# AV on the diagonal as two matmuls of half the queries, and router data laid out by expert, then tile

## The chip, the cores and the metric

The kernel runs on one core of a Trainium2 chip. The metric is the time of one execution on the device, in microseconds. Each core has a matrix engine (TensorE, PE in the profile, its weight loads PEld), a vector engine (VectorE, DVE), an engine for functions of one operand (ScalarE, ACT), GpSimd (POOL), which here issues most of the DMAs, and SyncE (SP), which issues the rest.

## The reference, cut to what matters

```python
# attention: batch 8, heads 8, seq 576, head_dim 64
block = 64
scores = scale * np.matmul(q, k.transpose(0, 1, 3, 2))
mask = pos[:, None] // block >= pos[None, :] // block     # causal by blocks of 64
scores = np.where(mask, scores, -1e9)
attn = softmax(scores);  x = attn @ v                      # -> 4608 tokens of 512
# mixture of 8 experts, two for each token
noisy_logits = x @ w_gate + np.log1p(np.exp(x @ w_noise)) * noise
top2 = np.argpartition(-noisy_logits, 2, axis=1)[:, :2]
out[t] = sum over its two experts e of  weight * (relu(x[t] @ w1[e]) @ w2[e])
```

Within a block of 64 queries everything is seen up to the block's own 64 keys. So in a diagonal square of 128 keys by 128 queries one quarter is masked: the later 64 keys against the earlier 64 queries.

## The kernel before, in words

The work has two stages. In the first, the attention of all heads and the routing are done; in the second, sixteen blocks of an expert's tokens run through the two layers.

**Attention.** The batches are taken in four groups `g` of two batches each; a batch is one half of the 128 partitions while scores are made (`hf`). A group has two sets `st` of four heads (`SET`). A set has thirteen score units (`score_unit`): a unit makes scores on TensorE (L299) in one of two PSUM buffers (`sc`) and turns them into exp values on ScalarE (L302), which go to the tile `esc`; the thirteenth makes the last 64 keys (L310, L313, `esc4`). Scores lie with the keys on the partitions and the queries along the row, so that `esc` is used as it is as the stationary operand of the AV matmul. For key tile `jt` of 128 keys, the columns from `EO[jt]` on hold the queries from that tile's first on. The first 128 of them are the diagonal square. Its masked quarter is partitions 64 to 127 by the first 64 columns, and `score_unit` clears it with four memsets on VectorE at the end of a set (L316).

**AV.** `av_tile` computes one tile of 128 queries for four heads, in one of two PSUM buffers (`av`): tile `idx` below 8 is batch `hf` and query tile `ib`, and sums `ib + 1` matmuls of 128 keys by 128 queries (L341), the last of them the diagonal one; the moving operand is the values with a column of ones (65 columns), so that the sum of the exps comes out as well. Tile 8 holds the last 64 queries of both batches, in halves of 64 columns (L352). VectorE then takes the reciprocal (L356) and multiplies (L357) into `xr`.

**Routing.** `x_transpose` turns `xr` (L373) and copies it (L374); `router` is a generator of sixteen steps: the logits (L388), exp, copy and log on ScalarE (L392 to L394), then a row of small VectorE operations that find each token's two experts (`oh`, L404 and L411), their mask `m` (L414), which of the two comes first (`ms`, L427 and L428), and by prefix sums a slot. Some of the small tiles are laid out with the nine token tiles outside and the eight experts inside (`p t e`), others, such as `oh_all` and `ms`, the other way (`p e t`), so some operations write or read with a step. `scatter` sends the rows to their slots in DRAM by indirect DMAs from GpSimd (L495).

**Order.** The order of the instructions on each engine is written out by hand (`tc.manual_schedule`). A loop over slots runs one score unit each (26 slots a group) and then what `at(slot, ...)` has put there. AV tiles of the first set of a group stand in slots 15 to 23 of that group, those of the second set in slots 0 to 8 of the next one (for the last group, in five slots close together after the end of the scores). Loads of q, k and v come from GpSimd's queue, in the same order.

**Experts.** `layer1` (L570, evicted at L573) and `layer2` (L582, L587, L592) run back to back over `SEQ`, with gathers (L610) and the output's scatter (L594) from GpSimd.

Of the kernel before, what the change touches and what calls it, by code (L numbers as in the profile page):

```python
# [8 lines left out]
F32 = mybir.dt.float32  # L9
BF16 = mybir.dt.bfloat16  # L10
I32 = mybir.dt.int32
AF = mybir.ActivationFunctionType
ALU = mybir.AluOpType
AX = mybir.AxisListType
# [5 lines left out]
def kernel(  # L20
# [12 lines left out]
    nc = tc.nc  # L33
# [3 lines left out]
    E = moe_w_gate.shape[1]  # L37
    F = moe_w1.shape[2]
    assert Dm == H * D and N == B * S
    P = 128  # L40
    DB = Dm // P
    FB = F // P
    NG = B // 2
    TG = 9
    NT = NG * TG
# [15 lines left out]
    EO = (0, 576, 1024, 1344)  # L61
# [29 lines left out]
    keep = ctx.enter_context(tc.tile_pool(name="keep", bufs=1))  # L91
# [10 lines left out]
    rt = low.enter_context(tc.tile_pool(name="rt", bufs=1))  # L102
# [26 lines left out]
    rowid_i = consts.tile([P, E, CT], I32)  # L129
    rowid = consts.tile([P, E, CT], F32)  # L130

    nz_all = keep.tile([P, NT, E], F32)
    xa = xa_pool.tile([P, DB, CAP], BF16)
    nzw = [xa.rearrange("p a b -> p (a b)")[0:B * TG, 1024 * i:1024 * (i + 1)].bitcast(F32) for i in range(2)]
    slots = keep.tile([P, NT, 2], I32)
# [149 lines left out]
    def score_unit(g, u):  # L285
        st, w = divmod(u, UN)
        if w == 0:
            escs[(g, st)] = (esc_pool.tile([P, SET, 2, ESC], BF16, tag="esc", name="esc"),
                             esc_pool.tile([P, SET, 64], BF16, tag="esc4", name="esc4"))
        esc, esc4 = escs[(g, st)]  # L290
        sc = sc_ps.tile([P, 2, 512], F32, tag="sc")
        if w < UN - 1:
            hh, piece = divmod(w, 3)
            h = st * SET + hh
            for jt, a, z, off in PIECES[piece]:
                for hf in range(2):
                    c0 = col0(hf, h)
                    sl = slice(64 * hf, 64 * hf + 64)
                    nc.tensor.matmul(out=sc[:, hf, off:off + z - a],  # L299
                                     lhsT=kT[sl, c0 + jt * P:c0 + jt * P + P],  # L300
                                     rhs=qT[sl, c0 + a:c0 + z], start=True, stop=True)
            ins = nc.scalar.activation(out=esc[:, hh, :, piece * 512:(piece + 1) * 512], in_=sc,  # L302
                                       func=AF.Exp, scale=scale)
        else:
            for hh in range(SET):
                h = st * SET + hh
                for hf in range(2):
                    c0 = col0(hf, h)
                    sl = slice(64 * hf, 64 * hf + 64)
                    nc.tensor.matmul(out=sc[sl, 0, hh * 64:(hh + 1) * 64],  # L310
                                     lhsT=kT[sl, c0 + 512:c0 + 576],
                                     rhs=qT[sl, c0 + 512:c0 + 576], start=True, stop=True)
            ins = nc.scalar.activation(out=esc4.rearrange("p a b -> p (a b)"), in_=sc[:, 0, 0:SET * 64],  # L313
                                       func=AF.Exp, scale=scale)
            for jt in range(4):
                nc.vector.memset(esc[64:128, :, :, EO[jt]:EO[jt] + 64], 0.0)  # L316
        anchors[g * UG + u] = ins.ins.name
        pace.append(ins.ins.name)

# [4 lines left out]
    def av_tile(g, st, idx, part=None):  # L324
        esc, esc4 = escs[(g, st)]
        vb = vt[g % 2]
        if g not in xrs:
            xrs[g] = xr_pool.tile([P, TG, DR], BF16, tag="xr", name="xr")
            nc.gpsimd.memset(xrs[g][:, :, Dm + 2 * NREC:DR], 0.0)
            nc.gpsimd.tensor_copy(xrs[g][:, :, Dm + 4:Dm + 6].bitcast(I32)[:, :, 0], tokm[:, g, :])  # L330
        xr = xrs[g]
        if part != 1:
            avs_open[idx] = av_ps.tile([P, SET, D + 1], F32, tag="av", name="av")
        av = avs_open[idx]
        for hh in (range(SET) if part is None else range(2 * part, 2 * part + 2)):
            h = st * SET + hh
            if idx < 8:
                hf, ib = divmod(idx, 4)
                for jt in range(ib + 1):
                    c = EO[jt] + (ib - jt) * P  # L340
                    nc.tensor.matmul(out=av[:, hh, :], lhsT=esc[:, hh, hf, c:c + P],  # L341
                                     rhs=vb[:, 4 * hf + jt, h, :], start=(jt == 0), stop=(jt == ib))
            else:
                for jt in range(5):
                    for hf in range(2):
                        sl = slice(64 * hf, 64 * hf + 64)
                        if jt < 4:
                            c = EO[jt] + (4 - jt) * P
                            lhsT, rhs = esc[:, hh, hf, c:c + 64], vb[:, 4 * hf + jt, h, :]
                        else:  # L350
                            lhsT, rhs = esc4[sl, hh, :], vb[sl, 8, h, :]
                        nc.tensor.matmul(out=av[sl, hh, :], lhsT=lhsT, rhs=rhs,  # L352
                                         start=(jt == 0), stop=(jt == 4))
        if part != 0:
            rden = small.tile([P, SET, 1], F32, tag="rden")
            nc.vector.reciprocal(rden, av[:, :, D:D + 1])  # L356
            ins = nc.vector.tensor_tensor(  # L357
                out=xr[:, idx, st * SET * D:(st + 1) * SET * D].rearrange("p (h d) -> p h d", h=SET),
                in0=av[:, :, 0:D], in1=rden.to_broadcast([P, SET, D]), op=ALU.mult)
            if g == NG - 1 and st == 1:  # L360
                pace.append(ins.ins.name)
# [19 lines left out]
    def router(g):  # L381
        half, t0 = g // 2, g * TG
        lg = av_ps.tile([P, TG, 2 * E], F32, tag="av")
        for idx in range(TG):
            if idx in (3, 6):
                yield
            for db in range(DB):
                nc.tensor.matmul(out=lg[:, idx, :], lhsT=xts[g][:, idx, db, :], rhs=wgn[:, db, :],  # L388
                                 start=(db == 0), stop=(db == DB - 1))
        sp = rt.tile([P, TG, E], F32, tag="sp")  # L390
        lgs = rt.tile([P, TG, E], F32, tag="lgs")
        nc.scalar.activation(out=sp, in_=lg[:, :, E:2 * E], func=AF.Exp)  # L392
        nc.scalar.activation(out=lgs, in_=lg[:, :, 0:E], func=AF.Copy)
        nc.scalar.activation(out=sp, in_=sp, func=AF.Ln, bias=1.0)  # L394
        yield
        noisy = rt.tile([P, TG, E], F32, tag="noisy")
        nc.vector.tensor_mul(noisy, sp, nz_all[:, t0:t0 + TG, :])
        nc.vector.tensor_add(noisy, noisy, lgs)
        yield
        mx = rt.tile([P, 2, TG, 1], F32, tag="mx")  # L400
        nc.vector.reduce_max(mx[:, 0, :, 0], noisy, axis=AX.X)
        oh = oh_all[:, g]
        ohv = [oh[:, i].rearrange("p e t -> p t e") for i in range(2)]
        nc.vector.tensor_tensor(out=ohv[0], in0=noisy, in1=mx[:, 0].to_broadcast([P, TG, E]),  # L404
                                op=ALU.is_equal)
        yield
        nc.vector.scalar_tensor_tensor(out=noisy, in0=ohv[0], scalar=-1.0e30, in1=noisy,
                                       op0=ALU.mult, op1=ALU.add)
        nc.vector.reduce_max(mx[:, 1, :, 0], noisy, axis=AX.X)
        yield  # L410
        nc.vector.tensor_tensor(out=ohv[1], in0=noisy, in1=mx[:, 1].to_broadcast([P, TG, E]),  # L411
                                op=ALU.is_equal)
        m = rt.tile([P, TG, E], BF16, tag="m")
        nc.vector.tensor_add(m.rearrange("p t e -> p e t"), oh[:, 0], oh[:, 1])  # L414

        w2 = rt.tile([P, TG], F32, tag="w2")
        nc.vector.tensor_sub(w2, mx[:, 0, :, 0], mx[:, 1, :, 0])
        yield

        c2 = rt.tile([P, TG, E], F32, tag="lgs")  # L420
# [2 lines left out]
                                     data1=m.rearrange("p t e -> p (t e)"), initial=0.0,  # L423
                                     op0=ALU.mult, op1=ALU.add)
        ms = rt.tile([P, 2, E, TG], BF16, tag="ms")
        msv = [ms[:, i].rearrange("p e t -> p t e") for i in range(2)]
        nc.vector.scalar_tensor_tensor(out=msv[1], in0=c2, scalar=2.0, in1=m, op0=ALU.is_equal, op1=ALU.mult)  # L427
        nc.vector.tensor_tensor(out=msv[0], in0=msv[1], in1=m, op=ALU.subtract)  # L428
        yield
        mf = ms.rearrange("p i e t -> p (i e t)")  # L430
        pp = av_ps.tile([P, 2, 2 * E * TG], F32, tag="av")
# [10 lines left out]
                                in0=incl.rearrange("p i e t -> p (i e t)"), in1=pp[:, 1, :], op=ALU.add)  # L442
# [231 lines left out]
    def spread_nz(eh, hf):  # L674
        e0 = eh * (E // 2)
        p = slice(64 * hf, 64 * hf + 64)
        src = rs["nz"][p].rearrange("p e (g b k) -> p e g b k", b=2, k=TG)
        dst = nz_all[p, :, e0:e0 + E // 2].rearrange("p (g i) e -> p e g i", i=TG)
        for bb in range(2):
            for e in range(E // 2):  # L680
                nc.vector.tensor_copy(dst[:, e, :, 4 * bb:4 * bb + 4], src[:, e, :, bb, hf:8:2])
        nc.vector.tensor_copy(dst[:, :, :, 8], src[:, :, :, hf, 8])
# [259 lines left out]
```

## Time and profile before

| | us |
|---|---|
| time, median of 3 (lowest, highest) | 455.42 (453.09, 455.93) |
| span of the profiled execution | 474.9 |
| PE busy | 419.3 |
| ACT busy | 253.2 |
| POOL busy | 249.4 |
| DVE busy | 162.0 |
| first matmul of the experts (L570) | at 173.0 |

The profiled execution is some 20 us longer than the timed ones. Busy time is the share of the span in which an engine has work recorded; a matmul's record goes on for about 200 ns after its start while the next one already starts, so that matmuls are compared by their starts. The granted clock (PEclk) is the share of TensorE's full clock that was granted; its records hold 1.0 and 0.5.

### The profile page before, as it was taken

How to read it: one execution, taken by the hardware profiler on the slowest of the kernel's cores; microseconds unless marked ns; L12 is line 12 of the kernel's file. 1: busy time of each engine (PE TensorE's matmuls, PEld its weight loads, DVE VectorE, ACT ScalarE, POOL GpSimd, SP SyncE). 2: the span in 40 equal slices, each digit the busy share in tenths (PEclk: the TensorE clock that was granted, in tenths of full speed). 3: DMA queues.
4: the chain of work that ended last, by engine and by line, in shares of the span. 5: the costliest groups of instructions: out<-in, count | busy, mean ns of one | idle time of the engine just before them, and what ended most of it. 6: DMA issues, size and time to landing. Idle time of an engine off the chain costs nothing.

```text
span 474.9 us, 9847 instructions
## 1 busy us (share of the span) xinstructions
PE 419.3 (88%) x3952; PEld 257.5 (54%) x3952; DVE 162.0 (34%) x508; ACT 253.2 (53%) x343; POOL 249.4 (53%) x297
## 2 busy tenths in 40 slices
PE   2899978869878478987999999999999989989994
PEld 2556755636545355554565565565566555555561
DVE  1677688576448537300210101101101202203212
ACT  2889897766567205443554455455455354454240
POOL 8877463378865456755210223435734736755433
PEclk9859999985975797998999999999999999999998
DMA  9999999979876935936993969978989989944222
GB/s 141 165 141 179 234 181 194 239 168 114 136 144 152 200 115 120 210 127 179 183 180 105 151 126 200 178 156 210 198 206 217 142 214 246 212 154 149 79 80 99
DMA packets 134633, 78.67 MB, mean 166 GB/s; under 512 B 96001, under 2 KB 124419, under 8 KB 134580
## 3 DMA queue, kind: packets, MB, share of 16 engines
q0 software_dynamic: 70368, 55.78, 71.6%
q1 hardware_dynamic: 54132, 13.00, 14.8%
q10 hardware_dynamic: 10080, 9.18, 6.0%
q8 instruction: 33, 0.54, 0.5%
q14 instruction: 20, 0.16, 0.1%
HBM read 68.28 MB, written 33.13 MB: 214 GB/s over the span
## 4 chain that ended last, share of the span: by engine, by line
PE 64%; ACT 8%; issue 7%; DVE 6%; another core or an unknown queue 5%; POOL 4%; DMA 4%; POOLq 0%; ACTq 0%; DVEq 0%
PE hp L570 25%; PE yp L582 24%; PE sc L299 4%; ACT esc L302 4%; PE av L341 4%; PE tp L256 3%; DMA yd<-ysb 2%; POOL out_dram L594 2%; DVE xr L357 2%; ACT hq L269 1%; PE av L352 1%; DMA raw<-in_k_dram 1%; POOL xd L495 1%; ACT hq L573 1%
## 5 line engine op out<-in xcount | busy, mean ns | idle before, releaser
L570 PE MATMUL hp<-xg,w1sb 128*128 128x320 bf16 x960 | 135.5, 301 | 8.2 <-ACT hq L573 8.1
L582 PE MATMUL yp<-w2sb,hq 128*128 128x512 bf16 x640 | 140.7, 379 | 0.0
L570 PEld LDWEIGHTS <-w1sb 128*128 128x128 bf16 x1024 | 101.6, 99 | 57.1 <-issue 13.8
L573 ACT ACTIVATE hq<-hp 128x640 bf16<-128x640 f32 x128 | 89.6, 704 | 68.3 <-PE hp L570 59.0
L592 DVE SCALAR_TENSOR_TENSOR yo<-yp,wrow,yg 128x512 f32<-128x512 f32 x46 | 34.5, 751 | 236.8 <-ACT ysb L587 192.0
L302 ACT ACTIVATE esc<-sc 128x1024 bf16<-128x1024 f32 x96 | 94.5, 1025 | 20.7 <-PE sc L299 16.1
L582 PEld LDWEIGHTS <-hq 128*128 128x128 bf16 x640 | 62.6, 98 | 73.0
L495 POOL DMA_INDIRECT xd<-xr,slots x72 | 71.2, 989 | 49.8 <-ACT esc L302 14.9
L610 POOL DMA_INDIRECT yg<-yd,orow x46 | 47.6, 1034 | 84.2 <-ACT hq L573 67.6
L587 ACT ACTIVATE ysb<-yp,wrow 128x512 bf16<-128x512 f32 x70 | 48.1, 687 | 75.5 <-PE yp L582 64.1
L594 POOL DMA_INDIRECT out_dram<-yo,trow x46 | 45.9, 997 | 61.3 <-DVE yo L592 46.2
L299 PE MATMUL sc<-hq 64*128 64x512 bf16 (+4 forms) x320 | 44.0, 346 | 11.5 <-ACT esc L302 9.4
L341 PE MATMUL av<-vt,esc 128*128 128x65 bf16 x640 | 35.6, 212 | 12.4 <-DVE xr L357 10.6
L341 PEld LDWEIGHTS <-esc 128*128 128x128 bf16 x640 | 27.8, 109 | 27.7 <-DVE xr L357 17.4
L212 POOL DMA_DIRECT2D vt<-in_v_dram x40 | 34.5, 875 | 8.6 <-PE av L352 5.5
L357 DVE TENSOR_TENSOR xr<-av,rden 128x256 bf16<-128x256 f32 x72 | 30.6, 425 | 2.7
L256 PE MATMUL tp<-ident,raw 128*64 128x128 bf16 x512 | 24.9, 251 | 2.8 <-DMA raw<-in_q_dram 1.6
L269 ACT ACTIVATE hq<-tp 128x1024 bf16<-128x1024 bf16 (+1 forms) x20 | 17.1, 854 | 17.7 <-PE sc L299 5.3
L299 PEld LDWEIGHTS <-hq 64*128 64x128 bf16 x320 | 13.1, 99 | 20.6 <-issue 12.6
L256 PEld LDWEIGHTS <-raw 128*64 128x64 bf16 x512 | 19.0, 128 | 7.8 <-issue 3.2
L356 DVE RECIPROCAL rden<-av 128x4 f32<-128x4 f32 x72 | 13.4, 187 | 18.0 <-PE av L341 5.2
L262 DVE COPY hq<-tp 128x1024 bf16<-128x1024 bf16 (+1 forms) x24 | 14.7, 611 | 11.4 <-PE tp L256 4.4
(122 smaller groups left out, 236.7 us busy)
## 6 DMA issues: line engine op xcount, KB each, us to landing
yd<-ysb ACTq DMA_DIRECT2D x70, 128.0 KB
w1sb<-in_moe_w_dram POOLq DMA_DIRECT2D x16, 512.0 KB
w2sb<-in_moe_w_dram POOLq DMA_DIRECT2D x16, 512.0 KB
vt<-in_v_dram POOLq DMA_DIRECT2D x32, 128.0 KB
raw<-in_q_dram POOLq DMA_DIRECT2D x9, 256.0 KB
raw<-in_k_dram POOLq DMA_DIRECT2D x9, 256.0 KB
xd<-zero SPq DMA_DIRECT2D x16, 132.0 KB
raw<-in_q_dram POOLq DMA_DIRECT2D x1, 1152.0 KB
```

Source lines behind the costliest of these rows:

```text
L256: nc.tensor.transpose(to[64 * hf:64 * hf + 64, :, r, :], raw[:, (t0, t1)[hf], r * 64:(r + 1) * 64], ident)
L299: nc.tensor.matmul(out=sc[:, hf, off:off + z - a], lhsT=kT[sl, c0 + jt * P:c0 + jt * P + P], rhs=qT[sl, c0 + a:c0 + z], start=True, stop=True)
L302: ins = nc.scalar.activation(out=esc[:, hh, :, piece * 512:(piece + 1) * 512], in_=sc, func=AF.Exp, scale=scale)
L341: nc.tensor.matmul(out=av[:, hh, :], lhsT=esc[:, hh, hf, c:c + P], rhs=vb[:, 4 * hf + jt, h, :], start=(jt == 0), stop=(jt == ib))
L357: ins = nc.vector.tensor_tensor(out=xr[:, idx, st * SET * D:(st + 1) * SET * D].rearrange("p (h d) -> p h d", h=SET), in0=av[:, :, 0:D], i ...
L495: ins = nc.gpsimd.indirect_dma_start(out=xd[half].bitcast(I32), out_offset=bass.IndirectOffsetOnAxis(ap=slots[:, g * TG + idx, i:i + 1], a ...
L570: nc.tensor.matmul(out=hp[:, n, 0:NW], lhsT=w1sb[:, db, fb * P:(fb + 1) * P], rhs=xgs[b][:, db, n * NW:(n + 1) * NW], start=(db == 0), sto ...
L573: ins = nc.scalar.activation(out=hs[b][:, fb, :].rearrange("p (n w) -> p n w", n=2), in_=hp[:, :, 0:NW], func=AF.Relu)
L582: nc.tensor.matmul(out=yp, lhsT=hs[b][:, fb, c * P:(c + 1) * P], rhs=w2sb[:, fb, :], start=(fb == 0), stop=(fb == FB - 1))
L587: ins = nc.scalar.activation(out=ysb, in_=yp, func=AF.Copy, scale=w)
L594: ins = nc.gpsimd.indirect_dma_start(out=out, out_offset=bass.IndirectOffsetOnAxis(ap=trow[half][:, e, c:c + 1], axis=0), in_=yo, in_offse ...
L610: ins = nc.gpsimd.indirect_dma_start(out=yg, out_offset=None, in_=yd[half][0:e * CAP, :], in_offset=bass.IndirectOffsetOnAxis(ap=orows[hal ...
```

## The change

The diagonal AV matmul is made two. The first takes the earlier 64 queries with the earlier 64 keys only; the second takes the later 64 queries with all 128 keys. Neither reads the masked quarter, so the memsets that cleared it go. The two write different halves of the partitions of the same PSUM tile; in both the accumulation ends.

In the router the tiles `sp`, `lgs`, `noisy`, `mx`, `nz_all` are laid out by expert, then token tile, as `oh_all` and `ms` already are, so that comparisons and products run with unit steps; `m` becomes float32 and keeps the order by tile, then expert, for the scan over experts. The maximum over experts is now read with a step, and so are the logits on ScalarE.

```diff
@@ score_unit
-            for jt in range(4):
-                nc.vector.memset(esc[64:128, :, :, EO[jt]:EO[jt] + 64], 0.0)
@@ av_tile
-                for jt in range(ib + 1):
+                for jt in range(ib):
                     c = EO[jt] + (ib - jt) * P
                     nc.tensor.matmul(out=av[:, hh, :], lhsT=esc[:, hh, hf, c:c + P],
-                                     rhs=vb[:, 4 * hf + jt, h, :], start=(jt == 0), stop=(jt == ib))
+                                     rhs=vb[:, 4 * hf + jt, h, :], start=(jt == 0), stop=False)
+                c, ks = EO[ib], vb[:, 4 * hf + ib, h, :]
+                nc.tensor.matmul(out=av[0:64, hh, :], lhsT=esc[0:64, hh, hf, c:c + 64], rhs=ks[0:64],
+                                 start=(ib == 0), stop=True)
+                nc.tensor.matmul(out=av[64:P, hh, :], lhsT=esc[:, hh, hf, c + 64:c + P], rhs=ks,
+                                 start=(ib == 0), stop=True)
@@ router
-        sp = rt.tile([P, TG, E], F32, tag="sp")
+        sp = rt.tile([P, E, TG], F32, tag="sp")
...
-        nc.scalar.activation(out=sp, in_=lg[:, :, E:2 * E], func=AF.Exp)
-        nc.scalar.activation(out=lgs, in_=lg[:, :, 0:E], func=AF.Copy)
+        lgv = lg.rearrange("p t e -> p e t")
+        nc.scalar.activation(out=sp, in_=lgv[:, E:2 * E], func=AF.Exp)
+        nc.scalar.activation(out=lgs, in_=lgv[:, 0:E], func=AF.Copy)
...
-        nc.vector.reduce_max(mx[:, 0, :, 0], noisy, axis=AX.X)
+        nc.vector.reduce_max(mx[:, 0, 0], noisy.rearrange("p e t -> p t e"), axis=AX.X)
...
-        nc.vector.tensor_tensor(out=ohv[0], in0=noisy, in1=mx[:, 0].to_broadcast([P, TG, E]),
+        nc.vector.tensor_tensor(out=oh[:, 0], in0=noisy, in1=mx[:, 0].to_broadcast([P, E, TG]),
                                 op=ALU.is_equal)
...
-        m = rt.tile([P, TG, E], BF16, tag="m")
-        nc.vector.tensor_add(m.rearrange("p t e -> p e t"), oh[:, 0], oh[:, 1])
+        m = rt.tile([P, TG, E], F32, tag="noisy")
+        mv = m.rearrange("p t e -> p e t")
+        nc.vector.tensor_add(mv, oh[:, 0], oh[:, 1])
...
-        nc.vector.scalar_tensor_tensor(out=msv[1], in0=c2, scalar=2.0, in1=m, op0=ALU.is_equal, op1=ALU.mult)
-        nc.vector.tensor_tensor(out=msv[0], in0=msv[1], in1=m, op=ALU.subtract)
+        nc.vector.scalar_tensor_tensor(out=ms[:, 1], in0=c2.rearrange("p t e -> p e t"), scalar=2.0, in1=mv,
+                                       op0=ALU.is_equal, op1=ALU.mult)
+        nc.vector.tensor_tensor(out=ms[:, 0], in0=ms[:, 1], in1=mv, op=ALU.subtract)
```

## Prediction

> **What bounds the kernel now.** I read the page's slices first, to find the stages, then the stretches of 20 us, then TensorE's order of time.
>
> ```profile
> PE   2899978869878478987999999999999989989994
> DVE  1677688576448537300210101101101202203212
> ACT  2889897766567205443554455455455354454240
> PEclk9859999985975797998999999999999999999998
> ```
>
> A slice is 11.9 us. TensorE is near full from the twentieth slice on: that is the expert stage, which starts at 173 us (the fifteenth slice), settles by 225, leaves VectorE and ScalarE half idle or more, and is not touched by the change. The change lies in the first fourteen or fifteen slices, where three engines share the load and the granted clock goes up and down. The stretches of that stage (columns: busy us and instructions of PE, PEld, DVE, ACT, POOL; granted clock; DMA share; GB/s):
>
> ```profile
> 40.00:60.00 20.00, 18.82 (x402) 13.71 (x399) 14.97 (x41) 17.62 (x24) 11.35 (x15) 1.00 1.43 215
> 60.00:80.00 20.00, 15.65 (x300) 10.55 (x300) 18.21 (x64) 17.16 (x21) 9.68 (x15) 1.00 1.80 183
> 80.00:100.00 20.00, 16.91 (x345) 12.02 (x342) 13.72 (x40) 15.44 (x20) 7.64 (x8) 1.00 1.08 233
> 100.00:120.00 20.00, 15.89 (x200) 9.84 (x199) 12.34 (x45) 12.21 (x16) 17.48 (x20) 0.58 0.98 112
> ```
>
> No engine is full all the time; TensorE has 15.7 to 18.8 of 20 us, ScalarE and VectorE up to 18. A busy TensorE is overstated, as a matmul's recorded end lies some 200 ns after its start, so I also took start-to-start times: an interval longer than the matmul's streaming time[...] plus the change of array grid priced below is idle. From 0 to 178 us that gives 121 us of work and 54 us of idle. By the exp that was running: the 68 stretches between exps that hold AV matmuls last 104 us with 20 us of idle; the rest of the idle lies in the start, in the stretches without AV, and at the end. What TensorE waits for from 20 to 178 us is short:
>
> ```profile
> PE av L341 <- DVE xr L357: 10.6, 9, 4.0
> PE sc L299 <- ACT esc L302: 8.5, 14, 2.0
> ...
> PE av L341 <- DVE esc L316: 0.3, 1, 0.3
> ```
>
> So the stage is a pipeline in which TensorE's own work comes first, with some 20 us of waits for the two banks of AV sums and for the exps. The waits for the memsets (L316) that the change removes are 0.3 us, and 1.4 us before weight loads.
>
> The price of the new matmuls is in the order of time (start, duration, count):
>
> ```profile
> 45.52 0.66 PE L341 MATMUL av<-vt,esc 128*128 128x65 bf16 x16
> 46.02 0.61 PE L373 MATMUL tp<-ident,xr 128*128 128x128 bf16 x8
> ...
> 51.09 0.86 PE L352 MATMUL av<-vt,esc 128*64 128x65 bf16 x20
> 51.88 0.62 PE L373 MATMUL tp<-ident,xr 128*128 128x128 bf16 x8
> ```
>
> Sixteen full AV matmuls take 0.50 us, 30 ns each. Twenty of the L352 matmuls take 0.79 us although they run in pairs: two start 3 ns apart, the next pair 29 ns later. The rest is lost where a head goes from 128 rows by 64 columns to 64 by 64 and back. Single starts there: 51.215, then 51.342 for the first 64*64 matmul (125 to 128 ns in all 25 cases at full clock), and 144 ns from the last 64*64 start to the next 128*64 start (14 cases). From a full 128*128 AV matmul to any smaller grid it is 121 to 128 ns.
>
> [...] 121 to 146 ns start to start where the grid changes, 30 ns where it doesn't. [...]the granted clock is 1.0 or 0.5 in every record, at half from 103 to 120 us[...] each memset is 64x256 uint32, 272 ns.
>
> **The change part by part.**
> *Diagonal matmuls.* Of 640 full AV matmuls, 256 (one for each of 8 x 8 x 4 head and query tile) become two: one 64*64, one 128*64. The order of the built program shows no other move on TensorE, and counts 264 changes of grid before, 918 after. Now one head of a tile with ib earlier key tiles, at full clock: before, ib+1 intervals of 30 ns. After: 125 (full to 64*64) + 144 (64*64 to 128*64) + 125 (back to full) + 30 (ib-1). The last step is not in the trace; it lies between 122 (the opposite step) and 146 (64*64 to full), and I take 125. Extra: 394 - 60 = 334 ns. With ib = 0: 144 + 126 - 30 = 240 ns. A half-group of four heads has 24 of the first kind and 8 of the second: 8.0 + 1.9 = 9.9 us, and eight of them 79 us. At half clock the trace has 54 ns for full to full and 173 for a change; 64*64 to 128*64 I put at 193. Extra 431 and 312 ns, 103 us in all. The AV stretches ran at a mean clock of 0.83, a third of the time at half: 0.67 x 79 + 0.33 x 103 = 87 us.
> *What of it is hidden.* The idle inside the AV stretches: VectorE's 0.6 us of normalization (L356, L357) gets a longer tile of matmuls to hide under, and exps run ahead. I let 14 of the 20 us go, and 4 of the 5.7 us that L341 waits for L357 in the last tiles (157 to 165 us). The idle of stretches without AV cannot be used: the order on TensorE is fixed and two score buffers carry little over.
> *Memsets.* 32 x 272 ns = 8.7 us leave VectorE. They precede rden and the transposes' copies on its queue, but TensorE's waits for them come to about 1 us. I count 1 us.
> *Router layout.* Five operations a group with a strided bf16 side take 477 to 502 ns (L404, L411, L414, L427, L428), the f32 ones of the same 72 elements 232 (L397). Unit steps should bring them near 232: 5 x 0.26 x 4 = 5 us. The two reduce_max now read with steps (229 ns before, at most about 500): up to 2 us back. Between them lie other steps of the queue, and behind them the scatters of a half; TensorE does not wait for these until the first experts. I count nothing; ScalarE's strided reads (L392, L393, 232 ns) are eight instructions.
> *Sum.* 87 - 14 - 4 - 1 = +68 us, in the attention stage alone: 455 + 68 = 523 us.
>
> **The rivals.**
> *The clock falls.* [...] AV stretches would stream less (a head with ib = 1 streams 3 x 27 of 394 ns), and the clock went to half at 130 us after 7 us in which TensorE streamed only about 40% of the time. Against: it stayed full from 35 to 103 us with stretches at 30%. With AV stretches all at half: 103, plus their own 83 us of work of which 55 ran at full and would take 1.8 times as long, +44, less 20 hidden: +127, 582 us.
> *Idle swallows more.* The timed runs are 20 us shorter than the profiled one, perhaps with less half clock; and DMA is at 9 tenths in the first eight slices, so loads may pace the stage. Against: TensorE's waits for raw are 2.3 us. All 20 us of AV idle, 6 of the tail and 9 of later stretches without AV are used, at full clock: 79 - 35 = +44, 499 us.
> *VectorE was the bound.* It has 18.2 of 20 us from 60 to 80, and 10.6 us of TensorE's waits are for its L357. If drains hide wholly in waits, the 13.7 us taken from VectorE give 10 us back: 445 us. Against: it needs 79 us of drains to fit in 54 us of idle, half of it at the wrong place.
>
> **How the numbers follow.** Forecast 0.58, clock 0.20, idle 0.15, VectorE 0.04; 0.03 for a cause not seen. The range goes from 490 (below the idle case) to 575 (between forecast and the clock case, most of which stays out): it leaves out some 0.19. Faster 0.04, same 0.02, slower 0.94.
>
> **What would show it.** TensorE's stage before the first L570 grows from 173 to about 240 us, the experts keep 17.3 us a block, and the waits av <- xr shrink below 3 us. The two new lines stand 120 to 150 ns from their neighbours. If they start some 30 ns apart, the step on drains is wrong and the whole sum falls; if the stage's mean clock drops below 0.7, the clock case holds; if VectorE's waits stay, the hidden share is wrong.

## The result, and the profile after

The changed kernel takes 576.5 us (571.0 to 587.1) against 454.3 for the kernel before: a ratio of 1.266, 95% interval 1.253 to 1.280. That is 122 us more, where 68 were forecast: the direction was right and the size not, and the time lies 1.5 us above the range. The profiles shown are each of an execution longer than the timed ones, by 20 us before and by 10 us after the change, so their spans differ by 110 us where the times differ by 122.

The page's slices of the changed kernel (585.3 us long, so a slice is 14.6 us):

```profile
PE   3799999999999998999989899999999999499995
DVE  1622324343343423432640020010011121011122
ACT  2934336342463425430345454555554545145530
PEclk9755557555575556555799899999999999899998
```

The experts start in the twentieth slice. From the third slice up to there TensorE is at 8 or 9 tenths; VectorE, mostly at 4 to 8 tenths before, is down to 2 to 4, and ScalarE, mostly at 5 to 9, to 2 to 6: the attention stage is bound by TensorE. The last row shows the other half of the story: the clock is at half for 246 of the 285 us before the experts. Four stretches of 20 us say it in numbers (columns as before the change: busy us and instructions of PE, PEld, DVE, ACT, POOL; granted clock; DMA share; GB/s):

```profile
60.00:80.00 20.00, 20.00 (x161) 12.48 (x160) 6.24 (x15) 6.05 (x7) 0.00 (x0) 0.50 0.20 62
100.00:120.00 20.00, 20.00 (x143) 11.87 (x141) 6.88 (x26) 7.25 (x9) 3.59 (x5) 0.51 1.36 188
140.00:160.00 20.00, 20.00 (x192) 12.88 (x188) 6.23 (x16) 7.60 (x8) 4.84 (x5) 0.50 0.20 70
200.00:220.00 20.00, 20.00 (x160) 12.57 (x161) 5.90 (x15) 6.03 (x6) 7.14 (x8) 0.50 0.30 68
```

TensorE is busy for 20 of 20 us with 143 to 192 matmuls, where 200 to 402 stood in such a stretch before. The reason is in the order of time of two heads of one tile (start, duration, line, grid, count):

```profile
61.75 0.24 PE L339 MATMUL av<-vt,esc 128*128 128x65 bf16 x1
61.91 0.26 PE L343 MATMUL av<-vt,esc 64*64 64x65 bf16 x1
62.10 0.26 PE L345 MATMUL av<-vt,esc 128*64 128x65 bf16 x1
62.30 0.23 PE L339 MATMUL av<-vt,esc 128*128 128x65 bf16 x1
62.46 0.26 PE L343 MATMUL av<-vt,esc 64*64 64x65 bf16 x1
62.65 0.26 PE L345 MATMUL av<-vt,esc 128*64 128x65 bf16 x1
```

Three matmuls make a head here, each on another grid, and their starts are 0.16 to 0.20 us apart; full ones follow each other every 0.03 us at full clock and 0.05 at half. The records do not show this time as idle: each lasts 0.23 to 0.26 us, past the next one's start, so TensorE counts as busy. This time from start to start at a change of grid is what the recorded texts call a drain; what the array does in it no trace shows. All waits of over 150 ns of TensorE from 20 to 285 us are these two; those for the AV buffers are gone:

```profile
PE sc L299 <- ACT esc L302: 7.2, 9, 1.5
PE tp L676 <- DVE hq L262: 0.6, 1, 0.6
```

By starts, and up to the first expert matmul: it comes at 284.8 us (173.0 before), with some 251 us of TensorE's work before it (119), the changes of grid included, and 28 us of idle (50); the split between the two depends by a few us on what is allowed for a change of grid. Behind it the kernels are alike, 300.5 and 301.9 us. In the profiles the whole loss lies in the attention stage.

### The profile page after: what moved, and what is told of

It is laid out like the page before. It is cut to its first block, busy times and chain, and to the rows that moved or that the text cites. A ratio compares the mean times of both kernels' runs of the same rounds, so it can differ in the third digit from the quotient of the medians.

```text
span 585.3 us, 10327 instructions
## 1 busy us (share of the span) xinstructions
PE 548.3 (94%) x4208; PEld 332.8 (57%) x4208; DVE 153.9 (26%) x476; ACT 256.4 (44%) x343; POOL 248.8 (43%) x297
## 5 line engine op out<-in xcount | busy, mean ns | idle before, releaser
L302 ACT ACTIVATE esc<-sc 128x1024 bf16<-128x1024 f32 x96 | 96.7, 1025 | 101.1 <-PE sc L299 100.7
L345 PE MATMUL av<-vt,esc 128*64 128x65 bf16 x256 | 66.7, 261 | 0.0
L343 PE MATMUL av<-vt,esc 64*64 64x65 bf16 x256 | 66.1, 258 | 0.0
L299 PE MATMUL sc<-hq 64*128 64x512 bf16 (+4 forms) x320 | 53.5, 414 | 9.3 <-ACT esc L302 8.1
L339 PE MATMUL av<-vt,esc 128*128 128x65 bf16 x384 | 55.9, 240 | 0.0
L343 PEld LDWEIGHTS <-esc 64*64 64x64 bf16 x256 | 31.8, 124 | 23.2 <-issue 3.8
L345 PEld LDWEIGHTS <-esc 128*64 128x64 bf16 x256 | 32.3, 126 | 16.4
L256 PE MATMUL tp<-ident,raw 128*64 128x128 bf16 x512 | 31.4, 291 | 2.9 <-DMA raw<-in_q_dram 2.6
```

What stands on the lines that cost most here:

```text
L299: nc.tensor.matmul(out=sc[:, hf, off:off + z - a], lhsT=kT[sl, c0 + jt * P:c0 + jt * P + P], rhs=qT[sl, c0 + a:c0 + z], start=True, stop=True)
L343: nc.tensor.matmul(out=av[0:64, hh, :], lhsT=esc[0:64, hh, hf, c:c + 64], rhs=ks[0:64], start=(ib == 0), stop=True)
L345: nc.tensor.matmul(out=av[64:P, hh, :], lhsT=esc[:, hh, hf, c + 64:c + P], rhs=ks, start=(ib == 0), stop=True)
```

## The experiments

Each run is compared with the kernel before, run beside it on the same chip. That kernel took 475 to 481 us in the first, second and fourth set of runs and 456 in the third. The third and the fourth set ran on one chip, so it is not the chip alone; the mean clock of the kernel before was higher in the third (0.953 against 0.931 to 0.936), but by the slopes given at the end of this section that makes less than half of the gap. The rest stays open, so ratios are given, and differences within one set. "Half" below is the time at half clock in the profile before the first expert matmul.

**Which part of the change.** The router's layout alone, and the half matmuls alone:

```diff
 e1_router: the full change, but
-                for jt in range(ib):   ... and the two half matmuls
+                for jt in range(ib + 1):   ... and the four memsets, as before
 e1_split: the kernel before, but with the two half matmuls and no memsets
```

> The router's new layout alone; the diagonal matmul and the memsets as before. If the lost time comes from the diagonal matmuls (drains, and the clock that falls with them): 448 to 457 us, VectorE some 5 us less busy. If steps in the new layout (reduce_max, ScalarE's strided reads) hold up the routing: a clear part of the 122 us, over 480.

> The two half matmuls alone, without memsets; the router's tiles as before. If the diagonal matmuls cost it all: 570 to 585 us, within 1% of the full change, mean clock in the first 280 us near 0.5. If the router has a share: well below 570.

The router's layout: 0.9947 (0.991 to 0.9985). The split: 1.231 (1.213 to 1.249). So the diagonal matmuls carry it. But the full change had stood at 1.266 in the first measurement, with an interval that does not touch this one, so both were run again side by side.

> The full change again, beside e4_split on one chip. If the router's layout neither costs nor gains once TensorE is the bound: within 1% of e4_split. If the layout costs something there (reduce_max with a step, on the way to the scatters): over 1% above e4_split, as the ratios from two chips (1.27 and 1.23) would have it.

> The two half matmuls alone, again, beside e4_full: within 1% of it if the diagonal matmuls are the whole loss; over 1% below it if the router's layout has a share.

Side by side: 1.241 (1.222 to 1.261) and 1.247 (1.229 to 1.264), 590.7 and 592.1 us. The split is the whole loss, some 111 us there; the gap between 1.27 and 1.23 came with the set of runs and not with the router.

**Number of matmuls, or changes of grid.** Two kernels pull them apart. In the first the heads of a tile go together, so that the same 4208 matmuls change grid 390 times instead of 918. In the second every AV matmul of tiles 0 to 7 becomes two of half the queries, 4592 matmuls in all, with 264 changes as before.

```diff
 e1_grouped4 (the loops only; the start and stop flags follow the new order)
-        for hh in range(SET):  full matmuls, one 64*64, one 128*64
+        for hh in range(SET):  full matmuls
+        for hh in range(SET):  one 64*64
+        for hh in range(SET):  one 128*64
 e1_pairs: the kernel before, but
+                    for lo in (0, 64):
-                    nc.tensor.matmul(out=av[:, hh, :], lhsT=esc[:, hh, hf, c:c + P], ...)
+                        nc.tensor.matmul(out=av[lo:lo + 64, hh, :], lhsT=esc[:, hh, hf, c + lo:c + lo + 64], ...)
```

> The full change, but the four heads of a tile go together: all full matmuls, then four of 64*64, then four of 128*64. The same 4208 matmuls of the same shapes as the full change; changes of grid 390 instead of 918 (264 before). If changes of grid cost it: 126 x 0.1 us of drains and 256 x 0.03 us of matmuls, some 20 us, of which 14 are hidden, and the clock recovers: 460 to 480 us. If the clock stays at half although the drains are gone: 500 to 515. If the number and the shape of the half matmuls cost it (more weight loads, half-empty array): near 576.

> Before, but every AV matmul of tiles 0 to 7 is made as two of 128 keys by 64 queries, side by side on the array; memsets as before. 640 more matmuls than before (the full change adds 256), changes of grid 264 as before. If changes of grid cost it: two run side by side, as in L352 (29 ns a pair): 450 to 462 us. If the number of matmuls and weight loads costs it: above 576, as 640 are more than 256.

The grouped kernel: 1.050 (1.032 to 1.068), +22 us. The pairs: 1.028 (1.019 to 1.037), +11 us, some more than expected. The number of matmuls is out as the cause: 640 more cost 11 us, the change's 256 more cost 111. Nor is it the shapes: the grouped kernel has the same ones. A tile of the grouped kernel in order of time:

```profile
61.06 0.42 PE L340 MATMUL av<-vt,esc 128*128 128x65 bf16 x8
61.41 0.31 PE L345 MATMUL av<-vt,esc 64*64 64x65 bf16 x4
61.65 0.32 PE L349 MATMUL av<-vt,esc 128*64 128x65 bf16 x4
61.90 0.62 PE L386 MATMUL tp<-ident,xr 128*128 128x128 bf16 x8
```

Sixteen matmuls of three grids take 0.84 us; four heads of that kind, one by one, make twelve changes of grid, and here there are three.

A kernel in between, with the heads two by two:

> As e1_grouped4, but the heads go together two by two: 566 changes of grid, the same 4208 matmuls. If the time goes with the number of changes, at the rate between the run with 390 (+22 us) and those with 918 (+110 to 122 us), 0.17 us each: +50 us on the kernel before, some 1.11 of it, the clock of the AV stretches between 0.72 and 0.51. If there is a point at which the clock drops for good: either near e1_grouped4 (1.05) or near the full change (1.2 and more).

1.142 (1.123 to 1.162), +64 us with 566 changes. Neither guess holds well: it is above the 50 us of the straight line and yet far from the full change. The series:

| kernel | changes of grid | us above before | half, us | clock of the AV stretches |
|---|---|---|---|---|
| before | 264 | 0 | 55 | 0.83 |
| e1_grouped4 | 390 | 22 | 92 | 0.72 |
| e2_grouped2 | 566 | 64 | 186 | 0.53 |
| e4_full | 918 | 110 | 249 | 0.52 |

The clock falls early in the series and is close to half from 566 on; the time goes on rising with the changes.

**Does the time lost at the changes of grid bring the clock down?** The test adds work that nobody uses: matmuls of 252 columns (some 105 ns each at full clock, an estimate from the experts' matmuls of 512 columns in the profile before, which start every 216 ns) into free columns of the tile's PSUM bank, ahead of each head. They bring 50 changes of grid with them, 968 in the traces.

```diff
 e2_filler1, e2_filler2, e3_filler3: the full change, with n = 1, 2, 3
+                for _ in range(n):
+                    nc.tensor.matmul(out=av_all[64:P, 260:512], lhsT=esc[:, hh, hf, EO[ib] + 64:EO[ib] + P],
+                                     rhs=vb[:, 4 * hf + ib] as 520 columns, the first 252, start=True, stop=True)
```

> The full change, with one more matmul of 252 columns ahead of each of the 256 heads' matmuls of tiles 0 to 7, 128*64 on the array, into columns of the PSUM bank that nobody reads; its result is not used. It adds nothing but streaming: 256 x 105 ns = 27 us at full clock, 54 us at half. If the clock is at half because the array streams too little in the AV stretches: it rises there, and the 27 us are more than paid back, 530 to 570 us against the 576 of the full change (1.17 to 1.25 of before). If the clock does not depend on it: +50 us, 1.35 and more.

> As e2_filler1, with two such matmuls for each head: 54 us of streaming at full clock, 108 us at half. If streaming decides the clock: the AV stretches at 0.8 and more, and still 540 to 600 us (1.19 to 1.32 of before). If not: 670 us and more (1.47).

One a head missed: the clock stayed at half, 649 us, 1.365 of before. With two, the profiled execution is shorter than with one, although it does 256 matmuls more, 601.6 us of span against 640.6. Stretches of 40 us, first of the kernel with one a head, then of that with two:

```profile
40.00:80.00 40.00, 39.23 (x314) 21.61 (x313) 8.85 (x24) 13.06 (x14) 6.49 (x9) 0.50 0.69 93
80.00:120.00 40.00, 39.78 (x384) 24.13 (x383) 12.84 (x37) 15.96 (x20) 12.05 (x16) 0.58 0.60 75
120.00:160.00 40.00, 39.23 (x307) 21.36 (x306) 11.43 (x41) 12.37 (x16) 3.59 (x4) 0.51 0.69 102
```

```profile
40.00:80.00 40.00, 39.17 (x443) 23.17 (x440) 11.84 (x34) 14.74 (x16) 7.58 (x11) 1.00 0.83 126
80.00:120.00 40.00, 38.69 (x498) 23.44 (x496) 16.23 (x51) 19.74 (x25) 13.55 (x18) 1.00 1.16 136
120.00:160.00 40.00, 37.88 (x514) 23.64 (x512) 16.45 (x46) 19.54 (x27) 14.53 (x15) 1.00 0.34 80
```

0.50 to 0.58 becomes 1.00, and TensorE gets through 443 to 514 matmuls where 307 to 384 stood. But the two timed executions lay at 603 and 645 us, so it was run again, beside three a head.

> The kernel of e2_filler2 again: its profiled execution had the clock at 0.86 before the experts and was faster than e2_filler1, the two timed ones lay 42 us apart. If streaming decides the clock and this amount lies near the point where it turns: times in two heaps, one near 600 us (clock held) and one near 645 us (clock fallen), or all near one of them. If the clock of that profile was chance: all near 645 us or above, clock below 0.7.

> The full change with three matmuls of 252 columns for each head, not used by anything. 27 us more of streaming than e3_filler2 at full clock, 54 us at half. If streaming decides the clock: it is held, above 0.86 in the part before the experts, 615 to 640 us in all executions. If not: 700 us and more.

Two a head: 612 to 631 us, between the heaps I had named rather than in them; the profiled execution spent 133 us at half (84 in the other one). Three: 630 to 638 us, 95 us at half, mean clock 0.86 before the experts. Without filler it is 0.57, and with one 0.55. So in these runs the clock was higher with two and three a head than with one or none, and two lie near the point where it turns.

The traces also show how much was enough. In the clock records of the kernel before, the first stretches of one clock last 3.41, 13.65, 68.27, 17.07 and 10.24 us, in those of the changed kernel 6.83, 71.68, 6.83 and 61.44 us: whole multiples of 3.41 us, as in all 18 profiles. The time before the experts was therefore divided into windows of that length, counted from those changes, and in each the share in which TensorE streams was taken by starts, whatever the grid (columns at 2.4 per ns at full clock, where matmuls of 512 columns start every 216 ns in the profile before, and at 1.2 at half, where those of 320 start every 267 ns).

In the kernel before and the changed one together, the 8 windows at full clock that a fall follows streamed for 0.13 to 0.39 of their time, the 27 others for at least 0.40. One window lies outside: the first recorded one of the kernel before, from 17.8 to 21.2 us, streamed for 0.46, and a fall follows. At half clock, the 9 windows that a rise follows streamed for at least 0.77, the 79 others for at most 0.75. All 18 profiles counted in this way, without that one window: at full clock 77 windows before a fall with at most 0.43, 421 others with at least 0.37; at half 68 before a rise with at least 0.72, 579 others with at most 0.77, but for one at 0.81. In these profiles the turn lay at some 2900 to 3500 columns a window in both cases (an estimate from these shares: 0.37 to 0.43 of 3413 ns at 2.4 columns per ns, 0.72 to 0.77 at 1.2), and at half clock nearly twice the share was needed to stream them.

So in these traces either state tended to last. In the profile of e2_filler2 the clock stayed full for 198 us with no window below 0.40 but the one that ended it, and then stayed at half for 82 us with none above 0.68. This fits the spread of the times of that kernel. In that of e2_filler1 the windows that stay at half reach 0.73, the lower edge of those that a rise follows.

The runs also give a rough size for each half of the loss. Where the clock was held (0.86 both times), the experts start at 304.7 us with two fillers a head and at 336.5 with three: 31.8 us for one. Taken down to none, that is 241 us: 68 above the kernel before, with the clock held. The 44 us from there to the 284.8 of the changed kernel would be the clock's. This is an estimate: a straight line through two profiles from two sets, whose kernels before differ by 4%, and with the 50 more changes of grid in it.

**A way back?** If changes of grid cost time, fewer than before should give some. Tile 8 has some of its own; its heads can be grouped two by two.

```diff
 e2_tile8: e1_router, and in tile 8
+            for hh in hhs:  the matmuls of 128 keys by 64 queries
+            for hh in hhs:  the two of 64*64
 e3_warm4, e3_warm2: e2_tile8, and ahead of every (every second) head of tiles 0 to 7
+                    nc.tensor.matmul(out=av_all[:, 260:512], ... 252 columns, not used)
```

> The router's new layout with the diagonal as before, and tile 8 (the last 64 queries) with its heads two by two: first their matmuls of 128 keys by 64 queries, then the 64*64 ones; 232 changes of grid instead of 264, the same matmuls. If each change costs as in the other runs: 32 x 0.1 to 0.17 us, 3 to 5 us below the router's layout alone, about 0.985 to 0.99 of before. If these drains lie beside other waits: no different from the router's layout alone (0.995).

> e2_tile8 with one matmul of 252 columns ahead of each of the 256 heads' matmuls of tiles 0 to 7, on the whole array, not used by anything: 27 us of streaming at full clock. Without the change's drains the clock is at half for 51 us before the experts. If streaming holds the clock: half-clock time below 25 us; the gain of some 15 us of work is eaten by what of the 27 us is not in idle time: 0.97 to 1.02 of before. If the clock is not held: 1.04 to 1.07.

> As e3_warm4, but ahead of every second head: 13 us of streaming. If streaming holds the clock already at this amount: 0.96 to 0.99 of before, below e2_tile8 (0.993). If not: 1.01 to 1.03.

> The router's layout alone, again, beside e4_tile8: 0.99 to 1.0 of before, as in e1_router (0.995).

> Tile 8 regrouped and the router's layout, again. If 32 changes of grid fewer count as in the other runs: 3 to 5 us below e4_router. If their drains lie beside other waits: no difference from e4_router, both some 0.5% below before.

Tile 8 regrouped: 0.993 (0.989 to 0.997), and 0.9976 (0.993 to 1.002) beside the router's layout alone at 0.9976 (0.993 to 1.002): no difference between the two. That the time at these changes lies beside other waits would fit, but no trace shows it. Both kernels stand at most 0.7% below before. With the fillers the clock stood higher there as well: 14 and 10 us at half before the experts in the profiles (51 in that of e2_tile8), with a mean clock of 0.96 and 0.97 there, and over the whole of the timed executions a mean clock of 0.985 and 0.973 where the kernel before had 0.953 beside them. But the times are 1.0025 (0.9997 to 1.005) and 0.998 (0.995 to 1.001) of before. Among the executions of the kernel before, one us less at half clock goes with 0.22 to 0.47 us less time, by set, and with 0.22 in this one. The 28 and 18 us less at half are then worth some 6 and 4 us, an estimate, and the added matmuls, 27 and 13 us of streaming at full clock (256 and 128 of the 105 ns estimated above), are enough to take that up. In the profiles the experts start at 163.2 and 159.5 us, and at 168.6 without fillers; but the last profile is from the second set, where the kernel before took 475 us and not 456, so this difference does not show a gain of the fillers.

## Why the prediction was wrong

**The step that failed** is the clock in the sum: "The AV stretches ran at a mean clock of 0.83, a third of the time at half", carried over to the changed kernel. They ran at 0.51. With 0.83 the extra work came to 87 us. By starts, the stretches with AV grew from 104 to 207 us although 13 us of idle went, so 116 us of work were added, the slower pace of the old work included. The prediction had named the sign of this case, a mean clock of the stage below 0.7; it was 0.57.

The rival "the clock falls" named what the profile shows, 0.51 in the AV stretches, and had 582 us against 576.5. That its sum is so close is in part luck: its +127 us meets the +122 of the times, while the stage in the profiles grew by 112. I gave it 0.20, since the clock had stayed full in stretches that streamed only 30% of the time. That was no evidence for a stage in which the changes of grid come everywhere. By windows of 3.41 us, the kernel before streamed for at least 0.40 of each from 35 to 100 us, and the clock fell after the next one, of 0.13; its later falls before the experts came after windows of 0.23 to 0.39, and its rises after 0.77 to 0.87. The prediction's own head of 3 x 27 in 394 ns (65 columns at 2.4 per ns are 27 ns) streams for 0.21. In the changed kernel the clock fell after windows of 0.22 to 0.35 and came back only after windows of 0.77 to 0.82; no other window at half reached 0.76.

**Changes of grid.** Right in kind, and a little low in size. The three steps of a head are 134, 144 and 150 ns at full clock (125, 144, 125 were used) and 175, 190 and 195 at half (173, 193, 173). The step back to the full grid was the one that the trace had not shown; its 150 ns (one case at full clock here, four in e4_full) are 4 ns above the upper bound named. With these the extra is 87 us instead of 79 at full clock and 108 instead of 103 at half; at the clock of 0.83 it would have been 94 instead of 87, so the size of these steps explains only 7 us of the miss.

**What is hidden.** 14 us of idle were said to go inside the AV stretches; it went from 20.4 to 7.4. TensorE's waits of over 150 ns for `xr` fell from 10.6 us to none.

**VectorE.** 13.7 us were to leave its queue; up to the experts its instructions took 126.4 us before and 112.7 after, 9.0 of it with the memsets (117.4 with the split alone), whose 32 records of 272 ns make 8.7. They bought nothing, as forecast. The router's rows before and then after, from the groups by form:

```profile
L404 DVE TENSOR_TENSOR oh_all<-noisy,mx 128x72 bf16<-128x72 f32 x4 | 2.0, 502 | 0.1
L414 DVE TENSOR_TENSOR m<-oh_all 128x72 bf16<-128x72 bf16 x4 | 2.0, 499 | 0.1
L401 DVE TENSOR_REDUCE mx<-noisy 128x9 f32<-128x72 f32 x4 | 0.9, 229 | 0.1
```

```profile
L408 DVE TENSOR_TENSOR oh_all<-noisy,mx 128x72 bf16<-128x72 f32 x4 | 0.9, 233 | 0.1
L419 DVE TENSOR_TENSOR m<-oh_all 128x72 f32<-128x72 bf16 x4 | 1.2, 291 | 0.1
L406 DVE TENSOR_REDUCE mx<-noisy 128x9 f32<-128x72 f32 x4 | 1.1, 281 | 0.1
```

`oh` fell from 502 ns to 233 as expected, `m`, which became float32 and where a step remains, from 499 to 291, and the maximum read with a step rose only from 229 to 281.

**The sum at a held clock** is supported, not shown: the fillers' line gives some 68 us, and the extra time of the changes of grid at full clock less the idle that went, 87 - 13, gives 74. That the first is the forecast's own number is chance, as the forecast had these changes 7 us too low and the line is rough. The main error was the choice of the case; the prices were near.

## What to carry to other kernels

Splitting a matmul to save masked work cost time here wherever a part did not have the grid of its neighbours: 134 to 150 ns from start to start at full clock and 175 to 195 at half, where 30 and some 50 stand on one grid. Putting the parts of one grid together brought 111 us down to 22; no split of these runs gained anything. Count the changes of grid in the order of the built program and read their price from starts, since the busy share does not show it: it was 20 of 20 us with 143 to 192 matmuls. And where a change makes TensorE stream less for its time, ask first whether the clock will hold, window by window; the mean clock of the kernel before, 0.83 in the AV stretches, was not the one to use, as they ran at 0.51 after the change.

## What was not expected of the hardware

Useless matmuls went with a shorter execution: 512 of 252 columns gave a profile of 601.6 us, where 256 of them gave 640.6 us. In the changed kernel the clock stayed at half for 51 to 72 us on end, four times, with hardly a wait of TensorE in the trace: those of over 150 ns come to 7.8 us from 20 to 285 us, the longest 1.5 us. None of its windows at half that streamed for 0.75 or less was followed by a rise, and all four falls in this stage came after windows that streamed for 0.22 to 0.35. And where both halves have one grid (128*64 in e1_pairs, eight such matmuls within 0.32 us), doubling the number of AV matmuls cost 11 us for 640 of them.
